# Folding a row maximum into the small operand: the max of k goes into v instead of into PSUM, in a linear-attention and channel-mix kernel

## The chip, the cores and the metric

The kernel runs on one core of one Trainium2 chip. The metric is the device time of one execution in microseconds (us). Only fast runs are compared; a run counts as slow when it is over 1.5% above the fastest of its kernel. A ratio in this document compares a kernel's fast runs with those of the kernel before in the same rounds on the same chip, so it isn't quite the ratio of the medians that stand beside it. Brackets hold its 95% interval.

## The reference, cut to what matters

```python
def phi(x):                                    # w_phi is 64 x 128
    proj = einsum('bhsd,df->bhsf', x, w_phi)
    proj = proj - max(abs(proj), axis=-1, keepdims=True)
    return concatenate([exp(proj), exp(-proj)], axis=-1)
q_p, k_p = phi(q), phi(k)                      # 8 batches, 8 heads, 576 positions
kv  = einsum('bhsf,bhsd->bhfd', k_p, v)
z   = sum(k_p, axis=2)
x   = (q_p @ kv) / (q_p @ z + 1e-06)           # then laid out as (batch, 576, 512)
# channel mix: xk, xr are mixtures of x and x shifted by one position
out = sigmoid(xr @ w_r) * (relu(xk @ w_k)**2 @ w_v)   # 512 -> 1024 -> 512
```

The line that matters is the sum over positions in kv. With m the row's maximum, the term is exp(±(p - m)) · v. That is exp(±p) · (exp(∓m) · v): the maximum can be subtracted before the large exponential, or multiplied into the 64 numbers of v (and the 1 that makes z) after it.

## The kernel before

The kernel is a list of small operations in one fixed order, the `ORDER` string. Two heads make a pair, and there are 32 pairs. Each engine takes its operations from the list in order, so an operation that waits holds up all those behind it on its engine. `/ENG` names the engine, `:n` the PSUM tile: three two-bank tiles (P) and two one-bank tiles (M). `+n@m` puts n dummy matmuls ("fills") there.

The names used below: `kp`, `qp` project k and q (TensorE); `rk`, `rq` take the maximum (VectorE); `mh` splits it into two bf16 numbers (GpSimd), `mt` transposes it, `mc` copies it out of PSUM; `ka` adds the maximum of k into k's PSUM tile by a matmul; `ea`, `eb` are the two large exponentials of k (ScalarE); `qt`, `qa`, `qb` do the same for q; `vc` copies v beside a column of ones; `kv`, `nd` are the two products; `rd` divides; `df`, `xa`, `xb` make the mixes (the difference, xk, xr); `h`, `r`, `v` are the channel mix's matmuls, with relu, square and gate between them.

```python
def rk():
    nc.vector.tensor_reduce(s["nm"][:, 0, :], s["k"]..., op=ALU.max,
                            apply_absolute_value=True, negate=True)
def vc(eng):
    copy(eng, v1s[b % 2][:, a, :, 0:64], vt[b][:, a, :]...)      # column 64 holds ones
def mhx():                                                       # q's and k's maximum together
    nc.gpsimd.tensor_copy(mhv[:, :, 0], nmv)
    nc.gpsimd.tensor_tensor(mhv[:, :, 1], nmv, mhv[:, :, 0], op=ALU.subtract)
def ka():
    for par in range(2):
        nc.tensor.matmul(s["k"][:, par, :], lhsT=s["mT"][r, :], rhs=sel[r, 0:4, :]..., start=False, ...)
def ek(pn):                                                      # ea: pn = 0, eb: pn = 1
    nc.scalar.activation(s[f"k{pn}"], s["k"]..., AF.Exp, scale=(1.0 if pn == 0 else -1.0))
# ... kv reads the same v for both signs:
    nc.tensor.matmul(ps[...], lhsT=s[f"k{pn}"][r, c, :], rhs=vb[r, a, 2 * g + par, :], ...)
# ... rd: reciprocal, and right behind it the multiplication by it
```

In the order a pair's k goes `kp rk mh mt mc ka ea eb`: a relay over TensorE, VectorE, GpSimd, TensorE, ScalarE or VectorE, TensorE and ScalarE.

Of the kernel before, what the change touches and what calls it, by code (L numbers as in the profile page):

```python
# [19 lines left out]
ones ident lv0.0 lv0.0.d:0 lk0.1 lq0.1 lv0.1 dve2 hk hq hk.d:0 lk0.1.d:0 dve3 hq.d:0 lk0.0.d/ACT  # L20
lq0.0.d/DVE lk0.2 lq0.2 pt0:2+9@0 wphi wphi.d:0 mus dve1 lv0.2 lk1.0 pb0/DVE pa0/ACT tr0 tp0.0:2+1@0
rt0.0 mhe0.0 lk0.2.d:0 qp0:1 rq0 lq0.2.d:0 kp0:0 rk0 mte0.0:1+3@0 lq1.0 lq1.0.d:0 lv1.0 mh0
lq0.1.d:0 pt1:1 pa1/DVE mce0.0/ACT kae0.0 lk1.2 lq1.2 lv1.2 pb1/ACT tr1 lq1.2.d:0 qp1:1+2@0 mt0:1
rq1 ekt0.0 mc0/ACT wk.0 pt2:2 ka0 pb2/DVE pa2/ACT kp1:1 rk1 mh1 ea0 pt3:2 pb3/ACT lk1.0.d:0 eb0
pa3/DVE tr3 mt1:1+4@0 mc1/DVE tr2 vc0/POOL wk.1 qp2:2 ka1 ea1 mus.d:0 eb1 rq2 kv0:0 kc0/DVE wr.0
wk.1.d:0 wr.1 lv1.2.d:0 kp2:2+1@0 rk2 wv.0 qt0:0 pt4:1+1@0 lv1.0.d:0 mh2 mt2:1+1@0 qa0 qb0 lk1.2.d:0
pa4/DVE pb4/DVE qte0.0:0 eqe0.0 tp0.1:1 mc2/DVE ka2 tr4 lv0.2.d:0 pt5:0 ea2 rt0.1 mhe0.1
mte0.1:0+1@1 pb5/DVE wv.0.d:0 pa5/DVE eb2 mce0.1/DVE kae0.1+2@1 lv0.1.d:0 ekt0.1 pt6:0 pb6/ACT
pa6/DVE pt7:2 pa7/DVE nd0:1 qt1:0 rd0 pb7/ACT vc1/POOL vc2/POOL vc3/ACT qp3:2 rq3 kp3:1+1@1 wv.1 rk3
mh3 tr6 qa1 qb1 tp0.2:2+3@1 qte0.1:0 tr7 eqe0.1 rt0.2 mhe0.2 kv1:0 kc1/ACT xt0:1 xf0/ACT mt3:0  # L30
mc3/ACT nd1:0 tr5 vc4/POOL xe0/ACT ka3 ea3 eb3 df0/POOL mte0.2:1+1@0 rd1 xt1:0 mce0.2/DVE kae0.2
ekt0.2 tp1.0:0 qte0.2:1 eqe0.2 rt1.0 qp4:1 qt2:2 lk2.0 qa2 qb2 mhe1.0 mte1.0:1 rq4 xa0 kv2:1 kc2/ACT
mce1.0/DVE kae1.0 ekt1.0 vc5/POOL xf1/DVE xb0 qte1.0:1 wr.0.d:0 kp4:2 kv3:1 eqe1.0 kc3/ACT nd2:0 rk4
mh4 mt4:1 rd2 qp5:1 mc4/ACT ka4 rq5 xe1/ACT wk.0.d:0 ea4 eb4 lq2.0 xt2:1 lq2.0.d:0 qp6:0 rq6
df1/POOL xa1 qt3:1+1@0 qa3 kv4:2+1@0 kc4/DVE wk.d xb1 wr.1.d:0 kp5:0 qt4:2+1@0 rk5 qb3 nd3:1 rd3 mh5
xe2/ACT mt5:0+3@0 lk2.0.d:0 tr2.0 xf2/ACT xt3:1 qa4 qb4 mc5/ACT df2/DVE ka5 xe3/ACT xf3/ACT tr2.2
xa2 xb2 wv.1.d:0 ea5 eb5 nd4:2 rd4 df3/POOL xa3 qt5:1 qa5 xb3 kv5:0+3@0 tr2.2.d:0 kp6:2 xt4:1
xf4/ACT xe4/DVE kc5/ACT h0.0:0 h0.1:1 qb5 rl0.0/ACT rl0.1/ACT sq0.0/ACT vc6/POOL vc7/DVE rk6 qp7:1
nd5:0 df4/POOL rq7 mh6 mt6:1 mc6/ACT h0.2:0 rl0.2/ACT qt6:1 qa6 xa4 tr2.0.d:0 wr.d r0.0:1 tr9 xb4
sq0.2/POOL th0.0 tr8 rd5 h0.3:0 qb6 sq0.1/POOL rl0.3/DVE lv2.0 lv2.0.d:0 xt5:1 xf5/DVE xe5/DVE ka6  # L40
kp7:0 h0.4:0 h0.5:1 qp8:1 ea6 df5/POOL eb6 rl0.4/ACT sq0.4/ACT rk7 mh7 sq0.3/ACT kv6:2 rl0.5/DVE
mt7:1 mc7/ACT lk3.0 lq3.0 lv3.0 lk4.0 lq4.0 rq8 lk4.0.d:0 kc6/ACT r0.1:0 th0.1 ka7 ea7 eb7 tr11 tr10
lq3.0.d:0 tp2.0:1 rt2.0 h0.6:1 r0.2:0 rl0.6/DVE sq0.6/ACT th0.2 nd6:2 rd6 h0.7:1 mhe2.0 mte2.0:0
mce2.0/DVE vc8/POOL vc9/POOL kv7:0 kc7/DVE rl0.7/ACT vc10/POOL kae2.0 ekt2.0 qp9:2 rq9 qte2.0:1
xt6:0 sq0.7/POOL qt7:0 lk3.0.d:0 xf6/DVE xe6/DVE eqe2.0 qa7 qb7 kp8:1 rk8 kp9:2 rk9 wv.d sq0.5/POOL
v0.0:0 ob0.0 tr3.0 so0.0 mh8 mt8:1 nd7:0 mc8/ACT ka8 mh9 mt9:0 mc9/ACT xa5 tr3.2 xb5 v0.1:1 rd7
ob0.1 tr3.2.d:0 vc11/ACT ea8 df6/POOL eb8 xa6 xb6 v0.2:0 ob0.2 xt7:1 xe7/ACT xf7/ACT qt8:1 qa8 qb8
df7/DVE xa7 xb7 ka9 lv3.0.d:0 vc12/POOL kv8:0 r0.3:0 tr3.0.d:0 tr13 tr12 lq4.0.d:0 th0.3 v0.3:1
kc8/DVE ob0.3 kp10:0 so0.1 qp10:1 rq10 rk10 ea9 eb9 h1.0:0 h1.1:1 rl1.0/ACT sq1.0/ACT nd8:1 rd8
kv9:2 kc9/ACT h1.2:0 qt9:1 qp11:2 mh10 rq11 rl1.1/ACT xz8 rl1.2/ACT sq1.2/POOL mt10:1 so0.2 mc10/ACT  # L50
sq1.1/POOL h1.3:0 rl1.3/DVE qa9 qb9 r1.0:1 th1.0 sq1.3/POOL kp11:2 rk11 mh11 ka10 ea10 h1.4:0 tr15
eb10 lv4.0 rl1.4/DVE sq1.4/ACT h1.5:1 rl1.5/DVE mt11:0 mc11/DVE so0.3 nd9:1 qp12:0 sq1.5/ACT ka11
xz8.d:0 ea11 eb11 h1.6:0 h1.7:1 vc13/POOL vc14/POOL tr14 vc15/POOL rd9 rq12 xz9 qt10:1 xz9.d:0
rl1.7/DVE rl1.6/DVE lk5.0 kv10:2 kc10/DVE tp3.0:0 sq1.7/POOL rt3.0 qa10 mhe3.0 qb10 r1.1:1 th1.1
he0.0:0 rle0.0/DVE nd10:1 r1.2:1 sq1.6/ACT mte3.0:0 mce3.0/ACT rd10 xz10 xz10.d:0 qt11:2 th1.2
kp12:1 xu8/POOL df8/DVE xa8 so0.0.d:0 kae3.0 xu9/POOL qa11 qb11 rk12 v1.0:1 ob1.0 mh12 ekt3.0
he0.1:0 mt12:1 mc12/ACT xb8 kv11:2 lv4.0.d:0 so0.1.d:0 tr4.0 df9/DVE rle0.1/ACT kc11/ACT qp13:0
qte3.0:1 sqe0.0/DVE eqe3.0 xu10/POOL df10/POOL ka12 kp13:2 so0.2.d:0 so0.3.d:0 so1.0 ea12 so1.0.d:0
r1.3:0 eb12 rq13 rk13 nd11:0 rd11 th1.3 v1.1:1 xz11 xz11.d:0 mh13 sqe0.1/ACT xa9 xb9 ob1.1 xa10 xb10
mt13:0 mc13/ACT kv12:0 kc12/ACT ka13 ea13 eb13 qt12:1 qa12 tr4.0.d:0 tr16 vc16/POOL xu11/POOL  # L60
df11/POOL qp14:0 rq14 v1.2:1 ob1.2 qb12 re0:0 the0 kp14:0 rk14 xa11 kv13:2 kc13/DVE so1.1 qt13:1
mh14 xb11 v1.3:0 tr4.2 tr4.2.d:0 tr19 vc17/POOL ob1.3 so1.3 mt14:1 qa13 nd12:2 qb13 mc14/ACT
vc18/POOL qp15:1 rq15 ka14 so1.1.d:0 ea14 so1.2 eb14 lq5.0 rd12 xz12 xz12.d:0 h2.0:0 rl2.0/DVE ve0:1
qt14:2 lq5.0.d:0 obe0 soe0 soe0.d:0 kp15:0 kv14:1 sq2.0/ACT qa14 qb14 lv5.0 lv5.0.d:0 vc19/DVE
h2.1:1 rk15 kc14/ACT h2.2:0 nd13:2 rd13 xz13 xz13.d:0 lk6.0 rl2.1/ACT sq2.1/POOL mh15 rl2.2/ACT
sq2.2/POOL r2.0:1 th2.0 tr18 h2.3:0 so1.3.d:0 mt15:1 tr17 qp16:2 qp17:1 mc15/DVE rl2.3/ACT lq6.0
lv6.0 ka15 ea15 eb15 h2.4:0 h2.5:1 rq16 rq17 sq2.3/POOL rl2.4/ACT xu12/POOL df12/POOL qt15:2 qa15
tp4.0:0 kv15:1 kc15/ACT h2.6:0 sq2.4/ACT rl2.5/DVE rt4.0 mhe4.0 rl2.6/DVE nd14:1 rd14 h2.7:1 qb15
vc20/POOL xa12 sq2.5/POOL lk5.0.d:0 xu13/POOL mte4.0:0 kp16:2 rk16 mce4.0/ACT kp17:1 rk17 kae4.0
mh16 rl2.7/ACT ekt4.0 r2.1:0 r2.2:1 th2.1 mt16:0 mc16/DVE xb12 xz14 df13/DVE nd15:0 so1.2.d:0 rd15  # L70
sq2.6/ACT xz15 sq2.7/ACT lq6.0.d:0 th2.2 mh17 ka16 ea16 xa13 v2.0:0 ob2.0 xb13 tr5.0 tr5.2 tr5.0.d:0
tr20 v2.1:1 eb16 mt17:0 mc17/ACT xz14.d:0 kv16:2 kc16/ACT ob2.1 vc21/POOL vc22/POOL qp18:0 rq18 ka17
ea17 qte4.0:1 xu14/POOL eb17 kp18:2 rk18 v2.2:0 eqe4.0 tr5.2.d:0 tr23 qp19:1 lk6.0.d:0 xz15.d:0
xu15/POOL df14/POOL xa14 qt16:0 qa16 ob2.2 r2.3:1 th2.3 mh18 v2.3:0 rq19 qb16 df15/POOL mt18:1
mc18/ACT kv17:1 so2.0 kc17/ACT xb14 ka18 ea18 eb18 qt17:0 qa17 qb17 nd16:1 xa15 xb15 h3.0:1 ob2.3
rd16 xz16 h3.1:0 rl3.0/DVE sq3.0/POOL so2.3 qp20:1 kp19:2 h3.2:1 rl3.2/ACT so2.2 rl3.1/DVE rk19
so2.2.d:0 r3.0:0 rq20 h3.3:1 th3.0 mh19 sq3.1/ACT sq3.2/POOL vc23/ACT rl3.3/ACT mt19:0 mc19/DVE
nd17:1 r3.1:0 th3.1 sq3.3/ACT so2.0.d:0 tr22 qt18:0 rd17 xz17 xz17.d:0 xz16.d:0 xu16/POOL qa18 qb18
ka19 ea19 df16/POOL xa16 kv18:1 kc18/DVE h3.4:0 rl3.4/DVE lk7.0 tr21 tp5.0:1 rt5.0 h3.5:1 sq3.4/DVE
rl3.5/ACT h3.6:0 rl3.6/DVE eb19 nd18:0 rd18 h3.7:1 mhe5.0 mte5.0:0 xz18 rl3.7/DVE sq3.5/ACT qt19:2  # L80
qp21:0 xu17/POOL rq21 mce5.0/ACT kae5.0 ekt5.0 sq3.6/POOL df17/POOL r3.2:1 th3.2 qte5.0:0 kv19:1
lv6.0.d:0 eqe5.0 kc19/ACT kp20:0 so2.3.d:0 xb16 he1.0:1 sq3.7/DVE v3.0:0 so2.1 xz18.d:0 so2.1.d:0
tr6.0 rk20 mh20 rle1.0/DVE qa19 qb19 xu18/POOL df18/POOL vc24/POOL mt20:1 mc20/DVE kp21:2 ka20
vc25/POOL ob3.0 so3.0 rk21 mh21 he1.1:1 rle1.1/DVE nd19:1 r3.3:0 rd19 xz19 xz19.d:0 mt21:1 ea20 eb20
xa18 qt20:0 mc21/ACT th3.3 qp22:1 xb18 qa20 lq7.0 rq22 ka21 v3.1:0 v3.2:1 ob3.1 kv20:1 qb20 xa17
xb17 ea21 eb21 so3.0.d:0 kc20/ACT ob3.2 so3.2 qt21:2 kv21:0 kp22:1 tr6.2 so3.1 re1:1 tr6.2.d:0
xu19/POOL df19/DVE xa19 sqe1.0/ACT xb19 tr27 rk22 mh22 v3.3:0 ob3.3 kc21/ACT nd20:0 rd20 sqe1.1/POOL
xz20 qa21 qb21 nd21:2 mt22:0 the1 tr6.0.d:0 h4.0:1 tr24 mc22/ACT ka22 ea22 rd21 qt22:0 so3.2.d:0
qa22 rl4.0/DVE ve1:0 eb22 vc26/POOL sq4.0/DVE lv7.0 r4.0:1 th4.0 tr25 obe1 qb22 so3.3 qp23:2 rq23
vc27/POOL xz21 kp23:1 rk23 h4.1:0 rl4.1/ACT xz20.d:0 h4.2:1 rl4.2/ACT h4.3:0 qp24:0 kv22:2 xz21.d:0  # L90
# [67 lines left out]
def kernel(  # L158
# [94 lines left out]
    def c_dve2():  # L253
        for t in mhls + mhlts:
            nc.vector.memset(t, 0.0)
# [716 lines left out]
```

## Time and profile before

| | before |
|---|---|
| median of 4 runs | 307.0 us (306.47 to 307.72) |
| span of the profiled run | 304.2 us |
| busy: TensorE, VectorE, ScalarE, GpSimd | 278.4, 240.3, 223.3, 127.4 us |
| chain: TensorE, VectorE, transfers, ScalarE | 61, 18, 7, 6% |
| last mixing step ends | 277.1 us |

In the views PE is TensorE, PEld its weight loads, DVE VectorE, ACT ScalarE, POOL GpSimd and SP SyncE. The busy line says how much of the span an engine executed something. The chain is followed backward from the last instruction, and says which engine each stretch of it lay on. The prediction shows these views.

### The profile page before, as it was taken

To read this page: it belongs to the slowest core of one execution; us is meant where nothing else is said; L and a number is where in the kernel's file an instruction comes from. 1 tells how busy PE (TensorE), PEld (TensorE's weight loads), DVE (VectorE), ACT (ScalarE), POOL (GpSimd) and SP (SyncE) were. 2 spreads that over 40 slices of the span, in tenths; PEclk is the share of its full clock that TensorE was granted. 3 is DMA by queue.
4 is the path that set the end of the run, shared out by engine and by line. 5 is a ranking of instruction groups with operands and counts; after the bars stand their busy time and mean duration, and the time that the engine had idled before them with its cause. 6 is when DMAs were issued, how large, how long until landed. Compare 5 with 4: busy or idle time off the path is not lost.

```text
span 304.2 us, 9054 instructions
## 1 busy us (share of the span) xinstructions
PE 278.4 (92%) x3765; PEld 158.4 (52%) x3813; DVE 240.3 (79%) x369; ACT 223.3 (73%) x408; POOL 127.4 (42%) x261
## 2 busy tenths in 40 slices
PE   6688798999899999969999997999999999999993
PEld 2456465565456655534555654454556655554541
DVE  5776789979978999667978988799869888777331
ACT  3397899998689897855888884898797878923410
POOL 7763533696047346653443714353034403400400
PEclk9999989999999999998999999999999999999999
DMA  8999957399989957996957898913924364233125
GB/s 152 204 209 207 169 83 105 59 194 206 194 174 128 148 124 131 197 200 113 177 110 107 145 125 157 162 47 61 187 60 69 11 93 94 58 74 71 39 58 116
DMA packets 66137, 38.18 MB, mean 126 GB/s; under 512 B 47024, under 2 KB 60720, under 8 KB 66096
## 3 DMA queue, kind: packets, MB, share of 16 engines
q1 hardware_dynamic: 51280, 20.82, 39.4%
q0 software_dynamic: 14672, 16.48, 35.1%
q8 instruction: 30, 0.49, 0.7%
q10 hardware_dynamic: 144, 0.29, 0.3%
q14 instruction: 11, 0.09, 0.1%
HBM read 33.62 MB, written 9.44 MB: 142 GB/s over the span
## 4 chain that ended last, share of the span: by engine, by line
PE 61%; DVE 18%; DMA 7%; ACT 6%; issue 3%; POOL 2%; SPq 1%; DVEq 0%; POOLq 0%
PE ps_v L812 14%; PE ps_h L779 13%; PE ps_r L798 7%; PE ps_nd L656 5%; DMA xs<-x_sc 4%; PE ps_kv L635 4%; DVE nm L565 4%; DVE nm L560 3%; DVE xk L706 2%; PE ps_ve L896 2%; ACT q L620 2%; PE ps_he L866 2%; DVE xr L706 2%; PE ps_q L548 2%; PE ps_k L598 2%
## 5 line engine op out<-in xcount | busy, mean ns | idle before, releaser
L620 ACT ACTIVATE q<-ps_qT 128x512 bf16<-128x512 f32 x128 | 67.1, 622 | 3.0 <-PE ps_qT L612 2.8
L575 ACT ACTIVATE k<-ps_k 128x1024 bf16<-128x1024 f32 x64 | 62.9, 1038 | 5.6 <-PE ps_k L598 4.3
L779 PE MATMUL ps_h<-xk,wk_bf 128*128 128x512 bf16 x237 | 60.8, 379 | 1.3 <-issue 0.3
L812 PE MATMUL ps_v<-wv_bf,kk 128*128 128x512 bf16 x243 | 58.2, 379 | 1.0 <-issue 0.3
L565 DVE TENSOR_REDUCE nm<-ps_q 128x8 f32<-128x1024 f32 x32 | 38.7, 1218 | 4.3 <-PE ps_q L548 4.1
L560 DVE TENSOR_REDUCE nm<-ps_k 128x8 f32<-128x1024 f32 x32 | 38.8, 1217 | 3.8 <-PE ps_k L548 3.8
L812 PEld LDWEIGHTS <-kk 128*128 128x128 bf16 x256 | 23.9, 98 | 28.8 <-issue 1.9
L211 POOL TENSOR_TENSOR kk<-krelu 128x512 bf16<-128x512 bf16 x23 | 23.9, 1047 | 35.4 <-DVE krelu L205 21.7
L779 PEld LDWEIGHTS <-wk_bf 128*128 128x128 bf16 x256 | 22.5, 97 | 25.2 <-issue 2.3
L584 POOL CAST mhl<-nm 128x16 bf16<-128x16 f32 x32 | 8.0, 250 | 64.1 <-DVE nm L560 64.0
L798 PE MATMUL ps_r<-wr_bf,xr 128*128 128x512 bf16 x118 | 32.9, 394 | 1.2 <-issue 0.5
L804 ACT ACTIVATE rt<-ps_r 128x512 bf16<-128x512 f32 x32 | 19.5, 609 | 18.0 <-PE ps_r L798 15.7
L700 POOL TENSOR_TENSOR diff<-xs 128x576 bf16<-128x576 bf16 x21 | 28.0, 1336 | 7.6 <-DVE xs L682 2.8
L203 ACT ACTIVATE krelu<-ps_h 128x512 bf16<-128x512 f32 x39 | 23.2, 611 | 10.1 <-PE ps_h L779 8.3
L706 DVE SCALAR_TENSOR_TENSOR xk<-diff,mu_k_t,xs 128x576 bf16<-128x576 bf16 x32 | 28.5, 892 | 1.3 <-POOL diff L700 1.0
L818 DVE SCALAR_TENSOR_TENSOR ob<-rt,ps_v 128x512 f32<-128x512 bf16 x32 | 21.8, 682 | 8.7 <-PE ps_v L812 4.2
L666 DVE TENSOR_TENSOR x_sc<-ps_nd,rden 128x640 bf16<-128x640 f32 x32 | 26.4, 825 | 1.1
L706 DVE SCALAR_TENSOR_TENSOR xr<-diff,mu_r_t,xs 128x576 bf16<-128x576 bf16 x32 | 26.9, 840 | 0.0
L548 PEld LDWEIGHTS <-qkT 64*128 64x128 bf16 x512 | 17.6, 94 | 12.0 <-issue 9.7
L635 PE MATMUL ps_kv<-v,k 64*128 64x65 bf16 x1024 | 22.8, 192 | 0.6 <-ACT q L620 0.4
L635 PEld LDWEIGHTS <-k 64*128 64x128 bf16 x1024 | 19.9, 95 | 5.1 <-issue 3.8
L205 DVE TENSOR_SCALAR krelu<-ps_h 128x512 bf16<-128x512 f32 x25 | 17.1, 688 | 6.6 <-PE ps_h L779 6.0
(99 smaller groups left out, 467.5 us busy)
## 6 DMA issues: line engine op xcount, KB each, us to landing
out_dram<-ob SPq DMA_DIRECT2D x72, 128.0 KB, 2.4
nat<-in_k_dram POOLq DMA_DIRECT2D x6, 576.0 KB, 8.6
nat<-in_q_dram POOLq DMA_DIRECT2D x6, 576.0 KB, 8.9
vt<-in_v_dram POOLq DMA_DIRECT2D x6, 576.0 KB, 9.6
wk_bf<-in_moe_w_k_dram POOLq DMA_DIRECT2D x2, 512.0 KB, 10.8
wv_bf<-in_moe_w_v_dram POOLq DMA_DIRECT2D x2, 512.0 KB, 12.3
nat<-in_k_dram POOLq DMA_DIRECT2D x3, 288.0 KB, 7.4
nat<-in_q_dram POOLq DMA_DIRECT2D x3, 288.0 KB, 7.3
```

What stands on the lines that cost most here:

```text
L211: (nc.vector if eng == "DVE" else nc.gpsimd).tensor_tensor(out_, in_, in_, op=ALU.mult)
L560: nc.vector.tensor_reduce(s["nm"][:, 0, :], s["k"].rearrange("p a (g f) -> p (a g) f", f=128), axis=AX.X, op=ALU.max, apply_absolute_value ...
L565: nc.vector.tensor_reduce(s["nm"][:, 1, :], s["q"].rearrange("p a (g f) -> p (a g) f", f=128), axis=AX.X, op=ALU.max, apply_absolute_value ...
L575: nc.scalar.activation(s[f"k{pn}"], s["k"].rearrange("p a (g f) -> p (a g) f", f=128), AF.Exp, scale=(1.0 if pn == 0 else -1.0))
L620: nc.scalar.activation(t[:, h, :].rearrange("f (g a p) -> f g a p", g=4, a=2), s["qT"].rearrange("f a (g h p) -> f h g a p", g=4, h=2)[:, ...
L635: nc.tensor.matmul(ps[:, hh, pn * 65:(pn + 1) * 65], lhsT=s[f"k{pn}"][r, c, :], rhs=vb[r, a, 2 * g + par, :], start=(pn == 0 and c == 0), ...
L666: nc.vector.tensor_tensor(s["x"].rearrange("p (b s) d -> p b s d", b=2), ndv[:, :, :, 0:64], s["rd"].to_broadcast([128, 2, 5, 64]), op=ALU ...
L700: (nc.vector if eng == "DVE" else nc.gpsimd).tensor_tensor(s["d"], xs[:, a, 64:64 + S], xs[:, a, 0:S], op=ALU.subtract)
L706: nc.vector.scalar_tensor_tensor(out=t[:, a, (b % 2) * S:(b % 2 + 1) * S], in0=s["d"], scalar=mu[:, a:a + 1], in1=xs[:, a, 0:S], op0=ALU.m ...
L779: nc.tensor.matmul(ps, lhsT=wk_bf[:, c, fc * 128:(fc + 1) * 128], rhs=xkt[bp][:, c, m0:m0 + 512], start=(c == 0), stop=(c == NDC - 1))
L798: nc.tensor.matmul(ps, lhsT=xrt[bp][:, c, m0 + ci * 128:m0 + (ci + 1) * 128], rhs=wr_bf[:, c, :], start=(c == 0), stop=(c == NDC - 1))
L812: nc.tensor.matmul(ps, lhsT=s["kk"][:, fc, ci * 128:(ci + 1) * 128], rhs=wv_bf[:, fc, :], start=(fc == 0), stop=(fc == NFC - 1))
```

## The change

The intent is to take `ka` out, so that k's exponentials follow straight on its maximum, and to give the work to GpSimd, the least loaded engine. Two tiny exponentials per pair (`em`, 8 columns) turn the negated maximum into the 65th column of v, and two multiplications per pair (`va`, `vb`) scale v by that column. The order was then made anew, by a model that knows that VectorE and GpSimd exclude each other at a shared port.

```diff
-        def mhx():                             # q's and k's maximum
+        def mhx(eng):                          # q's alone, depends on rq only
-        def ka(): ...                          # and kae, for the edge part
+        def em():
+            for pn in range(2):
+                nc.scalar.activation(vb[:, a, pn, 0:8, 64]..., s["nmk"]..., AF.Exp,
+                                     scale=(1.0 if pn == 0 else -1.0))
+        def vx(pn):                            # va: pn = 0, vb: pn = 1
+            def f(eng):
+                (nc.vector if eng == "DVE" else nc.gpsimd).tensor_tensor(
+                    vb[:, a, pn, :, 0:64], vt[b, a // 2][:, a % 2, :]...,
+                    vb[:, a, pn, :, 64:65].broadcast_to([128, R, D]), op=ALU.mult)
-        def vc(eng): ...
-                                         rhs=vb[r, a, 2 * g + par, :],
+                                         rhs=vb[r, a, pn, 2 * g + par, :],
+        def ra(): nc.vector.reciprocal(s["rd"], s["ndv"][:, :, :, 64])   # split off rd
-            t = get(vt, b, inp, [128, NP, X], BF, "vt")       # cast by the load, GpSimd's queue
+                t = get(vt, (b, c0 // 2), inp, [128, 2, X], FP, "vt", bufs=3)
+                (nc.sync if eng == "SP" else nc.gpsimd).dma_start(...)
-                ps = ptile(("P", f"pt{i}"), "ps_pt")          # first transposes: two banks
+                ps = motile(("mo", f"pt{i}.{bk}"), "ps_pt")   # one bank at a time
-ORDER = ...
+ORDER = ...                                    # new for the whole program
# (cut: engine choices of small copies, fills that may use a P tile, buffer counts)
```

The multiplication by a float32 v does the cast as well. That's what lets the loads of v leave GpSimd's queue: the Trainium skill's "DMA: Bandwidth & Descriptors", section SWDGE vs HWDGE vs iDMA, has the cast in a transfer as a thing of GpSimd's queue alone.

## The prediction

> **What bounds the kernel now.** I read the page's busy shares first, to see which engines could be the limit; then its slices, to see when; then the chain of waits, to see what a saved microsecond is worth; then the groups by shape and a timeline, for the cost of what the change touches.
>
> ```profile
> PE 278.4 (92%) x3765; PEld 158.4 (52%) x3813; DVE 240.3 (79%) x369; ACT 223.3 (73%) x408; POOL 127.4 (42%) x261
> ...
> PE   6688798999899999969999997999999999999993
> ...
> DVE  5776789979978999667978988799869888777331
> ACT  3397899998689897855888884898797878923410
> ```
>
> Three engines are loaded almost equally. Busy time flatters TensorE. Summing the trace's distances from one matmul's start to the next, and taking off every excess of more than 60 ns over its group's median, I find about 57 us without useful issue, so its work is about 304 - 57 = 247 us (81%), hardly more than VectorE's 240. There are three stages: a start (first 6 slices, 47 us) in which nothing is full because pairs wait on their own latencies; a long middle in which TensorE, VectorE and ScalarE are all near 80 to 90%; and from about 277 us a tail of 27 us, matmuls alone, after the last mixing step (last instruction of line 706 ends at 277.1 us).
>
> ```profile
> PE 61%; DVE 18%; DMA 7%; ACT 6%; issue 3%; POOL 2%; SPq 1%; DVEq 0%; POOLq 0%
> PE ps_v L812 14%; PE ps_h L779 13%; PE ps_r L798 7%; PE ps_nd L656 5%; DMA xs<-x_sc 4%; PE ps_kv L635 4%; DVE nm L565 4%; DVE nm L560 3%; DVE xk L706 2%; PE ps_ve L896 2%; ACT q L620 2%; PE ps_he L866 2%; DVE xr L706 2%; PE ps_q L548 2%; PE
> ```
>
> TensorE has 61% of the chain, 186 of its 247 us: work taken from it should be worth some three quarters of its length. VectorE has 55 of 240 us there, ScalarE 18 of 223, GpSimd 6 of 127.
>
> In the groups by shape, the rows that the change removes or that price what it adds (busy us, mean ns of one, then idle before):
>
> ```profile
> L598 PE MATMUL ps_k<-sel,mT 64*128 64x512 bf16 x64 | 12.7, 381 | 0.1
> ...
> L199 POOL COPY v<-vt 128x576 bf16<-128x576 bf16 x25 | 17.9, 740 | 0.0
> ...
> L700 POOL TENSOR_TENSOR diff<-xs 128x576 bf16<-128x576 bf16 x21 | 28.0, 1336 | 7.6 <-DVE xs L682 2.8 <-ACT xs L197 2.2 <-DVE xs L199 1.8
> ...
> L584 POOL CAST mhl<-nm 128x16 bf16<-128x16 f32 x32 | 8.0, 250 | 64.1 <-DVE nm L560 64.0
> ```
>
> The last row shows the dependency that goes: GpSimd stands 64 us waiting for the maximum of k. Behind it stands a relay for each head pair. From the timeline around 145 us (start, duration):
>
> ```profile
> 144.12 0.22 PE L589 MATMUL ps_m<-ident,mhl 128*128 128x128 bf16 x1
> ...
> 144.37 0.27 ACT L197 COPY mT<-ps_m 128x128 bf16<-128x128 bf16 x1 [1.89 <-PE ps_m L589]
> ...
> 145.05 0.38 PE L598 MATMUL ps_k<-sel,mT 64*128 64x512 bf16 x2
> ...
> 145.47 1.94 ACT L575 ACTIVATE k<-ps_k 128x1024 bf16<-128x1024 f32 x2
> ```
>
> The exponentials of k (1.94 us) wait for max, split, transpose, copy and a matmul that adds the max into PSUM; k's PSUM tile, one of only three two-bank tiles, is held all that time.
>
> **What the Trainium skill says.** "SBUF — State Buffer", section Who interferes with whom: a VectorE instruction with two SBUF inputs and a GpSimd instruction that reads SBUF take turns at a shared port; the later one blocks. The trace fits: the mix of line 706 mostly takes 0.81 us but up to 1.90, and the bf16 squares on VectorE are 0.42 us at best, 0.55 on average. Excess over typical values is (0.866 - 0.81) x 64 + (0.549 - 0.416) x 18 = 6 us of VectorE time. "GPSIMD Engine Reference", section 2.1: about 2.5 cycles an element for two inputs, so 1.2 us for 576 at its 1.2 GHz; line 700 takes 1.27 us undisturbed, which agrees. "ScalarE: Activation LUTs", section What ACT_TABLE_LOAD costs: 186 ns plus 0.833 ns an element, back-to-back ones overlapping by 93 ns; the trace's 63-column copy takes 226 ns (238 by the rule), and pairs of 1038 ns exponentials last 1.94 us together, so this agrees too.
>
> **The change part by part** (counts from the order of instructions of both kernels).
>
> TensorE loses the 64 max matmuls of k and the 10 of the edge. From start to next start these fill 10.4 and 1.6 us in the trace: 12.0 us, on the path for three quarters, 9 us. Warming fills go from 39 to 26; they sit in waits, so 0.
>
> ScalarE gains 84 tiny exponentials (64 of 8 columns, 20 of the edge). By the skill's rule one is 0.19 us, 0.10 where it overlaps: an estimate of 8 to 16 us. Moves between engines about cancel: nine more relus (+5.4) and twelve small copies (+2.5) against eight mT, two mTe and four v copies, four squares net of two edge ones, three kv copies and two qkT copies (about -8.5). Net about +11: 223 to 234 us. On the path at 18/223: +1 us.
>
> GpSimd loses 25 v copies (17.9), three quarters of the edge split (6), eight v-load issues (5.9), and some copies, differences and squares (12): 42 us. It gains 57 of the 64 multiplications of v by the two exponentials, priced like line 700 at 1.3 us: 74. Net +32, to about 159 us (53%). It doesn't become the bound; on the path at 6/127, +1.6 us.
>
> VectorE gets the other seven multiplications (0.66 us estimated from one element a cycle plus line 700's VectorE overhead: 4.6), eight mT copies (1.8), seven squares (3.4), 16 small splits (2.4), and about 4.5 of smaller copies; it sheds nine relus (6.2), three v copies (1.3) and the memset of v (0.2). About +9, to 249 us. On the path at 55/240: +2 us. The split-off reciprocal is the same 32 instructions of 0.215 us: 0.
>
> Latency: the relay on k's side shrinks to max, exponential (0.2 to 0.35), two multiplications on GpSimd (2.6), beside the big exponentials rather than ahead of them. About 1.3 us less per pair, and the PSUM tile is free some 2 us sooner. The split for q no longer waits for k's max. With the first transposes in one-bank tiles, I give the 47 us start 3 us.
>
> v now arrives as float32 on the sync queue, without the cast, in front of the DMA transposes of x. HBM reads are unchanged, so no bandwidth is lost, but a transpose behind a 590 KB load waits: +1.5 us. Against that, the middle of before has a hole (two transposes stuck for 8.9 us at 125 us, TensorE idle up to 2.6 us at a time); a new order may not have it: -2 us.
>
> Sum: -9 + 1 + 1.6 + 2 - 3 + 1.5 - 2 = about -8 us of 304.2: span 296.3. The clocked time is 3.1 us over the span, so 299.4; 299.5 us.
>
> **The rivals.** First, VectorE becomes the bound. For: it's already 79% busy and goes up by 9 us, while only TensorE is relieved. Before, it did about 231 us by the last mix at 277 us (83%). After, about 239 must be done by then (249 less some 10 of the tail). A tail of 25 us (one xr fewer ahead of it) and 83% would give 239/0.83 + 25 = 313 us of span: slower. Break-even needs 86%, a 2% gain 87.5%, a 4% gain 89.5%. Against: nearly all of VectorE's waits in the groups are for TensorE results (rden, nm, krelu, ob), which come sooner. I think 87 to 89% likely, and this is why my range reaches to 306.
>
> Second, the shared port. GpSimd's SBUF work grows by nearly half (96 to about 134 us without DMA issue), so 6 us of VectorE blocking could become 10 or more; but the order is made with that exclusion in it. Alone it would make about 303.
>
> Third, the schedule beats the parts: three stations no longer block each other, PSUM frees sooner, and the middle fills up. Then all 12 us of TensorE and 6 us of start come home: about 290 us.
>
> Fourth, TensorE's time was hidden after all and ScalarE's 84 small instructions delay the exponentials: 305 to 308, the same.
>
> **Range and chances.** The sum gives 299.5, just past the 2% line (301.1). Gains and losses of 8 to 10 us lie on both sides, so 291.5 to 307. Faster by over 2%: 0.56; within: 0.38; slower by over 2% (above 313.4), which needs VectorE not to get denser at all: 0.06.
>
> **What would show it.** TensorE busy lower by some 12 us and no ps_k matmul with sel; GpSimd 155 to 165 us with multiplications of 1.3 us (1.5 or more would mean port waits); VectorE 245 to 252, ScalarE 230 to 238; the chain with less TensorE and more VectorE; the fourth pair's x_sc before 44 us instead of 47.6; the last mix near 270. The prediction is wrong if the last mix stays at 277, if the mixes of line 706 and squares lengthen by over 4 us in total, or if TensorE waits for the folded v.

## More of the kernel before

One more is needed for later, the two mixing rows in the groups of before (busy us, mean ns of one, idle before):

```profile
L706 DVE SCALAR_TENSOR_TENSOR xk<-diff,mu_k_t,xs 128x576 bf16<-128x576 bf16 x32 | 28.5, 892 | 1.3 <-POOL diff L700 1.0
...
L706 DVE SCALAR_TENSOR_TENSOR xr<-diff,mu_r_t,xs 128x576 bf16<-128x576 bf16 x32 | 26.9, 840 | 0.0
```

## The result, and the profile after

| | before | after |
|---|---|---|
| median of 4 runs | 307.0 us (306.47 to 307.72) | 295.02 us (294.01 to 296.2) |
| ratio | | 0.9618 [0.9581, 0.9656] |
| span of the profiled run | 304.2 us | 292.1 us |
| fourth pair's divided result begins to be used: `x_sc` | 47.6 us | 39.1 us |
| the same for the eighth pair | 77.4 us | 77.4 us |
| mixes: an eighth done, half done | 52.6, 152.3 us | 47.4, 142.8 us |
| last mixing step ends | 277.1 us | 265.2 us |
| tail after it | 27.1 us | 26.9 us |

It is 12.0 us faster, all of it before the last mix. The page of the changed kernel, busy line and slices:

```profile
PE 263.4 (90%) x3681; PEld 154.6 (53%) x3726; DVE 250.2 (86%) x410; ACT 228.4 (78%) x492; POOL 160.5 (55%) x224
...
PE   6884867999999899998999999999798989899993
...
DVE  5993999899999799999998999999988996964421
ACT  3894997998999899898989958999777877723610
```

TensorE has lost 15 us of busy time and VectorE's row, which was full of sevens and eights, is now nines nearly up to the tail. The two traces cut at the last mix give the number: VectorE was busy 231.5 of 277.1 us before (84%) and 242.0 of 265.2 us after (91%). The chain of the changed kernel, by engine:

```profile
PE 47%; DVE 25%; DMA 11%; ACT 7%; issue 5%; POOL 3%; DVEq 0%; POOLq 0%; ACTq 0%
```

TensorE's share fell from 61% (186 us) to 47% (137 us), far more than the 12 us of work taken from it; VectorE's rose from 55 to 73 us. A chain regroups when a kernel changes. The groups by shape that answer to those of before:

```profile
L592 POOL TENSOR_TENSOR v<-vt,v 128x576 bf16<-128x576 f32 x57 | 69.4, 1230 | 22.5 <-ACT v L586 17.2 <-DMA vt<-in_v_dram 5.1
L728 DVE SCALAR_TENSOR_TENSOR xk<-diff,mu_k_t,xs 128x576 bf16<-128x576 bf16 x32 | 30.1, 952 | 0.1
L728 DVE SCALAR_TENSOR_TENSOR xr<-diff,mu_r_t,xs 128x576 bf16<-128x576 bf16 x32 | 29.3, 925 | 0.0
...
L586 ACT ACTIVATE v<-nmk 128x8 bf16<-128x8 f32 x64 | 11.2, 260 | 2.0 <-DVE nmk L574 2.0
L610 POOL CAST mhl<-nmq 128x8 bf16<-128x8 f32 x29 | 8.5, 294 | 14.7 <-DVE nmq L579 7.8 <-PE ps_k L561 3.7 <-DVE xs L704 2.5
```

GpSimd's wait for a maximum fell from 64.0 to 7.8 us in the split's row (its idle time in all from 64.1 to 14.7), and the multiplications of v wait 22.5 us instead, 17.2 of them for the tiny exponentials. There is no row of ps_k with sel any more. The mixes got longer: 952 and 925 ns in place of 892 and 840.

A pair's k in the middle of the changed kernel, from the timeline (start, duration; in brackets the idle time before):

```profile
143.50 1.22 DVE L574 TENSOR_REDUCE nmk<-ps_k 128x8 f32<-128x1024 f32 x1
...
144.75 1.94 ACT L600 ACTIVATE k<-ps_k 128x1024 bf16<-128x1024 f32 x2 [0.33 <-DVE nmk L574]
...
146.58 0.34 ACT L586 ACTIVATE v<-nmk 128x8 bf16<-128x8 f32 x2
...
146.99 1.18 POOL L592 TENSOR_TENSOR v<-vt,v 128x576 bf16<-128x576 f32 x1 [1.53 <-ACT v L586]
```

The maximum ends at 144.72 and k's exponentials start at 144.75. Nothing stands between them, where the prediction's timeline of before has transpose, copy and matmul. The tiny exponentials come behind the large ones here, and GpSimd waits 1.53 us for them.

The cost that the fold brings is seen in three lines around 165 us:

```profile
164.78 1.38 POOL L592 TENSOR_TENSOR v<-vt,v 128x576 bf16<-128x576 f32 x1 [5.45 <-ACT v L586]
165.05 1.72 DVE L728 SCALAR_TENSOR_TENSOR xk<-diff,mu_k_t,xs 128x576 bf16<-128x576 bf16 x1
...
168.05 0.82 DVE L728 SCALAR_TENSOR_TENSOR xr<-diff,mu_r_t,xs 128x576 bf16<-128x576 bf16 x1
```

A mix that begins while GpSimd multiplies takes 1.72 us, the next one, alone, 0.82. I summed the excess over the undisturbed duration for all VectorE instructions of that kind (mixes, differences, squares, v, small copies and splits): 6.2 us before, 14.7 us after, of which 11.0 us lie beside a multiplication of v.

Last, the start of the changed kernel has a hole:

```profile
22.91 0.76 POOL L324 DMA_DIRECT2D nat<-in_q_dram  x1 [1.78 <-DMA wk_bf<-in_moe_w_k_dram]
23.68 2.30 POOL L592 TENSOR_TENSOR v<-vt,v 128x576 bf16<-128x576 f32 x2
...
24.91 0.42 PE L652 MATMUL ps_kv<-v,k 64*128 64x65 bf16 x16 [3.44 <-POOL v L592]
...
27.97 0.22 DVE L681 RECIPROCAL rden<-ps_nd 128x10 f32<-128x10 f32 x1 [4.36 <-PE ps_nd L673]
```

TensorE waits 3.44 us for the second pair's v. Its multiplications stand in GpSimd's queue behind the issue of a load, which itself waits 1.78 us, by the profile for a weight load to land.

### The profile page after: what moved, and what is told of

Same layout as the page of the kernel before. It is cut to its first block, busy times and chain, and to the rows that moved or that the text cites. A ratio compares the mean times of both kernels' runs of the same rounds, so it can differ in the third digit from the quotient of the medians.

```text
span 292.1 us, 8998 instructions
## 1 busy us (share of the span) xinstructions
PE 263.4 (90%) x3681; PEld 154.6 (53%) x3726; DVE 250.2 (86%) x410; ACT 228.4 (78%) x492; POOL 160.5 (55%) x224
## 3 DMA queue, kind: packets, MB, share of 16 engines
q1 hardware_dynamic: 54688, 28.19, 47.6%
## 4 chain that ended last, share of the span: by engine, by line
PE 47%; DVE 25%; DMA 11%; ACT 7%; issue 5%; POOL 3%; DVEq 0%; POOLq 0%; ACTq 0%
PE ps_v L836 11%; PE ps_h L803 10%; PE ps_r L822 7%; DMA wk_bf<-in_moe_w_k_dram 5%; DMA xs<-x_sc 4%; DVE xk L728 4%; DVE xr L728 4%; PE ps_nd L673 4%; DVE nmq L579 4%; DVE nmk L574 3%; PE ps_kv L652 3%; ACT q L639 3%; DMA nat<-in_q_dram 2%; ACT k L600 2%; PE ps_ve L920 2%
## 5 line engine op out<-in xcount | busy, mean ns | idle before, releaser
L592 POOL TENSOR_TENSOR v<-vt,v 128x576 bf16<-128x576 f32 x57 | 69.4, 1230 | 22.5 <-ACT v L586 17.2
L639 ACT ACTIVATE q<-ps_qT 128x512 bf16<-128x512 f32 x128 | 68.9, 644 | 0.6 <-PE ps_qT L631 0.4
L579 DVE TENSOR_REDUCE nmq<-ps_q 128x8 f32<-128x1024 f32 x32 | 38.7, 1214 | 2.6 <-PE ps_q L561 1.9
L574 DVE TENSOR_REDUCE nmk<-ps_k 128x8 f32<-128x1024 f32 x32 | 38.8, 1215 | 1.8 <-PE ps_k L561 1.7
L836 PEld LDWEIGHTS <-kk 128*128 128x128 bf16 x256 | 24.1, 98 | 27.1 <-DVE xs L205 0.3
L209 ACT ACTIVATE krelu<-ps_h 128x512 bf16<-128x512 f32 x45 | 27.1, 606 | 7.5 <-PE ps_h L803 5.5
L728 DVE SCALAR_TENSOR_TENSOR xk<-diff,mu_k_t,xs 128x576 bf16<-128x576 bf16 x32 | 30.1, 952 | 0.1
L728 DVE SCALAR_TENSOR_TENSOR xr<-diff,mu_r_t,xs 128x576 bf16<-128x576 bf16 x32 | 29.3, 925 | 0.0
L217 POOL TENSOR_TENSOR kk<-krelu 128x512 bf16<-128x512 bf16 x20 | 21.2, 1066 | 8.1 <-DVE krelu L211 4.1
L561 PEld LDWEIGHTS <-qkT 64*128 64x128 bf16 x512 | 16.1, 94 | 11.8 <-issue 8.9
L673 PE MATMUL ps_nd<-kv,q 128*128 128x65 bf16 x512 | 22.2, 196 | 0.0
```

What stands on the lines that cost most here:

```text
L209: nc.scalar.activation(out_, in_, AF.Relu, scale=HALF)
L574: nc.vector.tensor_reduce(s["nmk"], s["k"].rearrange("p a (g f) -> p (a g) f", f=128), axis=AX.X, op=ALU.max, apply_absolute_value=True, n ...
L579: nc.vector.tensor_reduce(s["nmq"], s["q"].rearrange("p a (g f) -> p (a g) f", f=128), axis=AX.X, op=ALU.max, apply_absolute_value=True, n ...
L592: (nc.vector if eng == "DVE" else nc.gpsimd).tensor_tensor(vb[:, a, pn, :, 0:64], vt[b, a // 2][:, a % 2, :].rearrange("p (s d) -> p s d", ...
L639: nc.scalar.activation(t[:, h, :].rearrange("f (g a p) -> f g a p", g=4, a=2), s["qT"].rearrange("f a (g h p) -> f h g a p", g=4, h=2)[:, ...
L673: nc.tensor.matmul(ps[:, bk, o * 65:(o + 1) * 65], lhsT=tail if sl < 2 else s[f"q{pn}"][:, h, G * 128:(G + 1) * 128], rhs=s["kv"][:, h, pn ...
```

## The experiments

My theory: the gain is TensorE's shorter work, the shorter relay of k, and an order that packs the middle; the price is VectorE blocked at the port. The rivals: the removed matmuls alone explain it; the fold alone explains it and the new order is incidental; the order alone explains it and the matmuls were hidden.

Changes against the changed kernel itself are differences of two ratios, 0.9618 and the run's own, so each has the uncertainty of both, and the experiments were made on three chips.

### The matmuls put back

```diff
         # kp, behind the projection of k and before its maximum
+            for par in range(2):
+                nc.tensor.matmul(s["k"][:, par, :], lhsT=zw[r, :], rhs=sel[r, 0:4, :]..., start=False, ...)   # zw: zeros
```

> The changed kernel with the TensorE cost of the old max matmuls put back (two 512-column matmuls of zero weights per head pair right behind the projection of k, one per edge part), right result, no relay, same order. Theory 1 (the gain is the 12 us of TensorE work, three quarters of it on the path): about +9 us on the changed kernel, 303 to 305 us. Theory 2 (the gain is the shorter relay and the PSUM tile freed sooner): +0 to 3 us, 295 to 298. Theory 3 (the gain is the new order): +0 to 3 us, 295 to 298.

Measured: correct, 300.1 us (298.0 to 301.33), ratio 0.9806 [0.9742, 0.987].

```profile
PE 276.2 (92%) x3800; PEld 159.3 (53%) x3800; DVE 255.3 (85%) x411; ACT 229.3 (77%) x492; POOL 160.8 (54%) x224
...
L737 DVE SCALAR_TENSOR_TENSOR xk<-diff,mu_k_t,xs 128x576 bf16<-128x576 bf16 x32 | 31.3, 987 | 0.1
L737 DVE SCALAR_TENSOR_TENSOR xr<-diff,mu_r_t,xs 128x576 bf16<-128x576 bf16 x32 | 30.6, 967 | 0.0
...
L574 PE MATMUL ps_k<-sel,zw 64*128 64x512 bf16 x64 | 12.8, 376 | 0.0
```

The 12.8 us of matmuls are back in the row, and 0.9806/0.9618 is 1.95%, 5.8 us (about 3.5 to 8 with both intervals). So at most about half of TensorE's 12 us is on the path in the new order. The 5.8 us is rather too much than too little: the matmuls also lie in front of the maximum, where `ka` did not, and the order shifts against the port. The mixes took 987 and 967 ns in this run (952 and 925 in the changed kernel), and VectorE's busy time rose by 5.1 us, to 255.3, though its work is all but the same. How much of the 5.8 us that is wasn't separated.

### The matmuls taken out of the old order

```diff
-... mc0/ACT wk.0 pt2:2 ka0 ... ea0
+... mc0/ACT wk.0 pt2:2 ... ea0          # all ka and kae gone, nothing in their place
```

> The kernel before with only the max matmuls of k and of the edge taken out, wrong result on purpose: the exponentials of k no longer wait for the relay, TensorE has 12 us less, everything else and the order as before. Theory 1 and theory 2 together: 9 to 12 us faster than before, 295 to 298 us. Theory 3 (order): 0 to 3 us faster, 304 to 307 us, because other waits in the old order hold it.

Measured: wrong (the maximum of k isn't subtracted; relative error 0.020), 303.25 us (300.3 to 307.14; one run slow, and the profile with it), ratio 0.99 [0.9831, 0.9969]. In the old order the matmuls, and the wait of k's exponentials for the relay, were worth 3 us (1 to 5). The rival that the removed matmuls explain the 12 us falls.

### The fold alone, in the old order

```diff
-... mc3/ACT ... ka3 ea3 eb3 ... vc3/ACT
+... mc3/ACT ... em3 ea3 eb3 ... va3 vb3   # loads, transposes and reciprocal as before
```

> The fold alone in the old order: max matmuls out, tiny exponentials in their places, the two multiplications of v in the place of the old copy of v (or just behind the exponentials), loads of v as before, transposes and reciprocal as before; right result. Theories 1 and 2: close to the changed kernel, 294 to 298 us. Theory 3: little or no gain, 302 to 309 us, as GpSimd gets 42 to 50 us of work in an order that was not made for it.

Measured: correct, 348.66 us (345.2 to 351.88), ratio 1.1331 [1.1258, 1.1403], granted clock 0.931 in the profiled run, which was slow. From its page and its waits (engine and line waited for; us in total, times, longest):

```profile
PE 288.2 (83%) x3739; PEld 163.1 (47%) x3739; DVE 248.5 (71%) x370; ACT 228.6 (66%) x488; POOL 177.0 (51%) x274
```

```profile
POOL v L577 <- ACT v L571: 65.3, 20, 8.4
```

The fold by itself costs 13%. GpSimd stands 65 us waiting for tiny exponentials, because I had put them at `ka`'s places, behind the whole relay, and all else on GpSimd's in-order queue waits with it.

### The fold in the old order, better placed

```diff
-... rk3 ... em3 ea3 eb3
+... rk3 em3 ... ea3 va3 vb3 eb3           # em right behind the maximum, the edge's likewise
```

> The fold alone in the old order once more, better placed: tiny exponentials right behind the maxima they read, the multiplications of v right behind the first big exponential of k, rest as e3_fold_only (348 us); right result. If the waits of GpSimd for the tiny exponentials (65 us in e3_fold_only) made its loss: 300 us or less. If the old order as a whole doesn't suit the fold: 310 us or more.

Measured: correct, 356.97 us (356.23 to 359.37), ratio 1.1676 [1.1624, 1.1728], granted clock 0.925. From its waits:

```profile
ACT v L572 <- DVE nmk L560: 41.5, 23, 4.6
...
POOL v L578 <- ACT v L572: 24.0, 12, 3.3
```

The wait that I removed from GpSimd (65 to 24 us) turned up on ScalarE (41.5 us waiting for the maximum), and the kernel got slower still. Behind the relay GpSimd waits, right behind the maximum ScalarE does. Two tries don't show that no place in the old order would do. But in both the fold alone makes the kernel slower, so the rival that the fold explains the gain and the order is incidental falls. What each of the many waits adds to the 51 us (16.8% of 306) was not separated, nor what the lower clock adds.

### Multiplications cut to 4 of 64 columns

```diff
-                    vb[:, a, pn, :, 0:64], vt[...]..., ....broadcast_to([128, R, D]), op=ALU.mult)
+                    vb[:, a, pn, :, 0:4], vt[...]...[:, :, 0:4], ....broadcast_to([128, R, 4]), op=ALU.mult)   # from batch 3 on
```

> The changed kernel with the multiplications of v cut to 4 of 64 columns from the third batch on (48 of 64 of them), wrong result on purpose: takes some 45 us of GpSimd's and most of the port blocking on VectorE away. If GpSimd's work and the port (VectorE's mixes lost 8 us in 64 instructions) are on the path: 3 to 6 us faster than the changed kernel, 289 to 292 us. If the order hides them: within 1.5 us, 293.5 to 296.

Measured: wrong, 288.92 us (287.54 to 289.06), ratio 0.9453 [0.941, 0.9495]: 1.7%, 5 us less than the changed kernel.

```profile
L730 DVE SCALAR_TENSOR_TENSOR xk<-diff,mu_k_t,xs 128x576 bf16<-128x576 bf16 x32 | 26.0, 823 | 0.1
...
L594 POOL TENSOR_TENSOR v<-vt,v 128x36 bf16<-128x36 f32 x41 | 13.1, 329 | 25.8 <-ACT v L586 19.9 <-DMA vt<-in_v_dram 5.9
```

GpSimd's busy time fell to 120.6 us, and the mixes are back at 823 and 841 ns. This doesn't tell whether the 5 us came from GpSimd's time or from the port.

### The same time on GpSimd, without its reads

```diff
+                if b >= 2 and eng == "POOL":      # from batch 3 on
+                    nc.gpsimd.memset(vb[:, a, pn, :, :], 0.02)
+                    nc.gpsimd.memset(vb[:, a, pn, :, :], 0.01)
+                    return
```

> The changed kernel with GpSimd's multiplications of v from the third batch on replaced by two fills of the same output (no SBUF read; about the same 1 to 1.3 us of GpSimd each, and the same order of waits), wrong result on purpose. e4_small_mult took time and reads away and gained 5 us. If the port (GpSimd reading while VectorE reads twice) is what costs: near e4_small_mult, 0.945 to 0.952 of the kernel before, and VectorE's mixes back near 0.84 us. If GpSimd's time is what costs: near the changed kernel, 0.958 to 0.965.

Measured: wrong, 289.24 us (287.82 to 290.04), ratio 0.9445 [0.9404, 0.9485], as the run with 4 columns.

```profile
L732 DVE SCALAR_TENSOR_TENSOR xk<-diff,mu_k_t,xs 128x576 bf16<-128x576 bf16 x32 | 26.4, 835 | 0.1
...
L593 POOL MEMSET v<- 128x585 bf16 x41 | 24.1, 587 | 17.1 <-ACT v L586 17.0
```

Two fills of 587 ns hold GpSimd for 1.17 us, as long as an undisturbed multiplication, and write the same output, but read nothing. GpSimd is busy 154.2 us, nearly as in the changed kernel; VectorE's blocked time falls from 14.7 to 7.3 us. The fills don't wait for v's load, which the multiplications do for 5.1 us; but the run with 4 columns kept that wait (5.9 us) and gained the same. So about 5 us of the changed kernel's time is the port, not GpSimd's length. This agrees with the Trainium skill's "SBUF — State Buffer", section Who interferes with whom, in both its halves: a GpSimd instruction that only writes does not block the two-input mixes (835 ns), one that reads does (952 ns).

### The loads of v on GpSimd's queue

```diff
-lv2.0/SP ... lv2.2/SP ...
+lv2.0/POOL ... lv2.2/POOL ...             # all of them, same places in the order
```

> The changed kernel with all loads of v issued by GpSimd, as in the kernel before, instead of 13 of 17 on the sync queue; float32 as in the change. If v's loads delay the DMA transposes on the sync queue (my +1.5 us): 1 to 2 us faster, 293 to 294. If GpSimd's 13 more issues of about 0.75 us (10 us) sit before multiplications that are waited for: 2 to 6 us slower, 297 to 301.

Measured: correct, 304.04 us (301.78 to 305.98), ratio 0.9932 [0.9891, 0.9974]: 3.3%, about 10 us more than the changed kernel. Its chain, and a mixing row:

```profile
PE 35%; DVE 31%; DMA 11%; POOL 7%; issue 7%; ACT 4%; SPq 2%; DVEq 0%; POOLq 0%; ACTq 0%
...
L728 DVE SCALAR_TENSOR_TENSOR xk<-diff,mu_k_t,xs 128x576 bf16<-128x576 bf16 x32 | 31.9, 1008 | 0.8 <-POOL diff L722 0.7
```

Thirteen issues come to GpSimd, of 0.69 us each in the changed kernel's trace and 0.73 in this one's; its busy time rose by 8.6 us, from 160.5 to 169.1. VectorE's blocked time rose from 14.7 to 25.4 us and its busy time to 261.0. I take it that late multiplications collide with the mixes they had been placed around. The move of the loads is thus a large part of what the order needs; that they cost 10 us in another order made for them isn't shown.

### The reciprocal joined again, and four first transposes back in two banks

```diff
-... ra1 va2/POOL ... qt2:0 em3 rd1
+... va2/POOL ... qt2:0 em3 ra1 rd1
```

> The changed kernel with each reciprocal moved back to right before its multiplication, as in the kernel before. My prediction gave the split 0 us. If it is only bookkeeping: within 1 us of the changed kernel, 294 to 296. If the split lets VectorE do other work while the result settles: 1 to 3 us slower, 296 to 298.

Measured: correct, 296.62 us (293.03 to 297.5, one slow), ratio 0.9648 [0.9599, 0.9698]: no difference from the changed kernel that can be told.

```diff
-                ps = motile(("mo", f"pt{i}.{bk}"), "ps_pt")
+                ps = st["ps", i][:, bk, :]        # pairs 0, 1, 2 and 4, in a free two-bank tile
```

> The changed kernel with four of the eight first transposes (pairs 0, 1, 2, 4, where the new order leaves a tile free) back in the two-bank tiles. If the one-bank tiles only made room for the order: within 1 us of the changed kernel. If they are faster by themselves at the start: 1 to 3 us slower.

Measured: correct, 294.51 us (292.51 to 301.87, one slow), ratio 0.9606 [0.9564, 0.9648]: none either. The other four pairs can't be tried, as no two-bank tile is free at their places in the new order. That the order could only be made with one-bank tiles stays possible.

### The tiny exponentials twice

```diff
-            for pn in range(2):
+            for pn in (0, 1, 0, 1):
```

> The changed kernel with the 64 tiny exponentials of the pairs done twice: +11 us of ScalarE. If ScalarE is off the path (7% of the chain, some 9% of its work): +1 us, 295 to 297. If ScalarE at 78% has become a bound: +4 us or more, 299 and over.

Measured: correct, 297.73 us (293.28 to 306.05), but four of six runs were slow; the two fast ones give 0.962 [0.9564, 0.9676]. ScalarE's busy time rose to 236.3 us (in a slow profile). As far as two runs tell, 8 us more of ScalarE costs nothing. But the four are slow by their time alone, and three of them ran at clocks of 0.986 to 0.989, as the fast ones did (0.991 and 0.979); so a cost of some 2 us isn't ruled out.

### The hole of the start closed

```diff
-... ea1 wk.1 ... mt2:1 em1 qte0.1:0 ... eb2 va1/POOL pb4/DVE ... vb1/POOL kp3:1
+... ea1 em1 wk.1 ... qp3:0 va1/POOL vb1/POOL lk2.0 ... eb2 pb4/DVE ... kp3:1
```

> The changed kernel with the tiny exponentials of the second pair moved forward on ScalarE and its two multiplications moved in front of the third batch's load of k on GpSimd's queue. In the trace they stand behind a load of q whose issue waits until 22.9 us for an earlier load to land, and TensorE is idle from 21.5 to 24.9 us. If that hole is on the path: 2 to 3 us faster, 292 to 293. If later waits take it up: within 1 us.

Measured: correct, 291.59 us (289.35 to 293.01), ratio 0.9512 [0.947, 0.9555], 1.1% or 3 us below the changed kernel: better than both kernels.

```profile
17.27 2.31 POOL L592 TENSOR_TENSOR v<-vt,v 128x576 bf16<-128x576 f32 x2
...
21.92 0.42 PE L652 MATMUL ps_kv<-v,k 64*128 64x65 bf16 x16 [0.34 <-DVE nmq L579]
```

The second pair's v is multiplied at 17.3 us instead of 23.7, ahead of the two load issues, and the product starts 3 us earlier. This gain at the start lasts to the end.

```diff
-... lk2.0 lk2.0.d ... lq2.0 lq2.0.d pt4.1:0 ...
+... lk2.0 lk2.0.d ... pt4.1:0 ... vb3/POOL lq2.0 lq2.0.d ...    # on top of the former
```

> e8_start_fix with the third batch's load of q moved behind the multiplications of the fourth pair: its issue held GpSimd until 22.5 us in e8_start_fix, with the splits of q's maxima behind it. If these are waited for: 1 us faster than e8_start_fix, 0.945 to 0.949 of the kernel before. If not: 0.950 to 0.953.

Measured: correct, 291.77 us (288.56 to 296.0, two slow), ratio 0.9488 [0.9437, 0.9539]. Moving the waiting load issue away as well isn't told apart from the former.

## Why the prediction was right or wrong

The direction and the size held: 8 us less predicted, 12.0 measured, within the range. The reasons held in part, and that the sum came so near is partly luck: the sum hoped for too much of TensorE and left the port out, and against both stands the move of the loads of v, which it had counted as a loss.

**TensorE, 9 us.** The work is 12 us as worked out (12.8 us in the row of the run that puts it back), but three quarters of it on the path was too much: at most 5.8 us in the new order, 3 us in the old. The step that failed is the reading of the chain: a share of 186 of 247 us was taken as what a saved microsecond brings. The 247 was also too low. It came from gaps between matmuls, and both traces lack some 45 matmul records, among them 19 or 20 of 256 in ps_h, which look like about 10 us of idle time. With 257 the same rule would give 8.7 us; still too much. When the work shrank by 12 us, TensorE's part of the chain shrank by 49, and others took its place.

**ScalarE, +1.** The 84 tiny exponentials are busy 14.4 us in all, within the 8 to 16 estimated; ScalarE's total of 228.4 us lies just under the 230 to 238 named as a sign. Doubling 64 of them showed no clear cost.

**GpSimd, +1.6, and VectorE, +2.** Busy times came out as counted: 160.5 us (155 to 165), 250.2 us (245 to 252). A multiplication takes 1.23 us on average and 1.17 undisturbed, against 1.3; on VectorE it takes 0.89, against 0.66. VectorE's fit is luck: of the 9.9 us by which it rose, 8.5 are blocked time, which the count of 9 had left out. GpSimd's count has a slip, too: it loses seven load issues (11 before, 4 after), not eight. What these terms missed is the port: the mixes alone lengthened by (952 - 892 + 925 - 840) × 32 = 4.6 us, and about 5 us of the time is the port. My sign of being wrong, over 4 us for mixes and squares together, wasn't quite reached, as the squares got shorter (549 to 472 ns): 2.7 us in all. The prediction had the port as a rival, with 6 us of blocked time growing to 10 or more. It's 14.7, and the gain stood all the same.

**The start, -3.** The mixes' first eighth is 5.2 us earlier, the fourth pair's result 8.5 us (39.1 us, before the 44 named). The eighth pair's is level again, so this lead was spent elsewhere; it isn't clear how much of it the end keeps. The one-bank tiles, to which I had given it, show nothing for the four pairs that could be tried.

**v on the sync queue, +1.5.** For the move as a whole the sign was wrong. I counted a transpose behind a load, and the issues that GpSimd loses only as time at the small weight that GpSimd has on the chain, not for what stands behind them in its queue. With all loads of v on GpSimd the kernel takes 10 us more in this order. The delay itself isn't seen: the 24 transposes of x land after 3.5 us at the median in both kernels, and after 3.9 with all loads of v on GpSimd.

**The hole of the middle, -2.** Not tested. The changed kernel has a stuck transpose as well, 8.84 us at 87.8 us.

**The latency, counted in no term of its own.** The trace shows k's exponentials 0.03 us behind the maximum. Its worth was not measured alone.

**A sign that came true.** "TensorE waits for the folded v" was to show that the prediction is wrong, and it does: 4.6 us in total, 3.44 of them in the hole of the start. Moving that hole's multiplications forward brought 3 us on top of the gain.

**The rivals.** The first, VectorE as the bound, set the break-even at 86% of density and the 4% gain at 89.5%; the trace has 91%, and without the blocked time (242.0 - 14.7) / 265.2 = 86% against (231.5 - 6.2) / 277.1 = 81% before. So VectorE did get denser, more than the 87 to 89% thought likely. The third, "the schedule beats the parts", came closest: the parts put back one by one in the new order cost 5.8 us (matmuls), 10 us (loads' queue) and nothing that can be told (reciprocal, transposes), the fold alone in the old order costs 13 to 17% in place of a gain, and the removal alone is worth 3 us. They don't add up to 12 us: what a part is worth depends on the rest. But not all of TensorE's 12 us came home, as that rival had it. The fourth, hidden TensorE time, was right by half.

What stays open: which waits make the fold so costly in the old order; what an order without the port exclusion in its model would have given, which I couldn't make; and the rival of the order alone. No new order was made for the kernel without the fold, so how much of the 12 us it would have brought isn't known.

## What to carry to other kernels

A step that can be moved from a large operand to a small one can be worth moving even if at most half of the busy engine's relief comes home; here it also took a relay out of k's chain, whose worth was not measured. In a statically ordered program such a change must be judged with an order made for it: the same fold, in two placements, cost 13 to 17% in the old order and was part of a gain of 4% in the new one. Before trusting a share of the chain as the value of a saving, put the work back with dummy instructions and measure; and when GpSimd gets new work beside a busy VectorE, compare a version that only writes, which shows what the shared port takes.

## What the Trainium skill lacked or had wrong

- "SBUF — State Buffer", section Who interferes with whom, has the rule and it held, but no size for a whole kernel. Here 57 reading GpSimd multiplications of 1.2 us brought VectorE's blocked time from 6.2 to 14.7 us, and cost about 5 us of 295.
- "Trainium Kernel Development and Optimization", section Key Constraints, says that issuing transfers from several engines only saves the sequencer's issue time. The saving isn't small here: 13 loads of v more or less on GpSimd's queue are 8.6 us of GpSimd's busy time and, in this order, 10 us of the kernel's, with VectorE's blocked time between 14.7 and 25.4 us.
- "ScalarE: Activation LUTs", section What ACT_TABLE_LOAD costs: its rule gives 0.19 us for an 8-column activation; the trace has 0.26 us on average, 0.34 for a pair back to back (0.29 by the rule with its overlap).
